# Half of a wo stripe moved ahead of the last V piece and projected there, in a decode-attention kernel

## The chip, the cores and the metric

One core of one Trainium2 chip. The metric is device time in microseconds (us) of one execution; lower is better. "Span" below is the time from the first to the last instruction of an execution; it is 1.2 to 1.6 us (at times up to 2.4 us) shorter than the device time of the same execution, and it was recorded for every run of the experiments.

## The reference

Two independent problems, A and B, of the same shape: one new token per batch row (B = 2), 32 query heads, 16 K/V heads, head size 128, model size 576, a cache of 16384 positions of which only the last W = 4096 count. Everything is bf16.

```python
q = (x @ wq).reshape(B, Sq, Hq, Dh).transpose(0, 2, 1, 3)
k = jnp.repeat(k_cache[:, :, Sk - W:, :], 2, axis=1)
v = jnp.repeat(v_cache[:, :, Sk - W:, :], 2, axis=1)
p = softmax(einsum("bhqd,bhkd->bhqk", q, k) * Dh ** -0.5)
o = einsum("bhqk,bhkd->bhqd", p, v)
out = o.transpose(0, 2, 1, 3).reshape(B, Sq, Hq * Dh) @ wo      # [2, 1, 576]
# the result is A's and B's out, side by side: [2, 1, 1152]
```

The matrix products are tiny, the caches are not: 153 MB have to be read.

## The kernel before

All K and V windows stream through a ring of four 4 MB slots, one slab per (problem, group of four K/V heads, batch row): K slab t, then V slab t - 3, and the pieces of `wo` between them. All large transfers are issued on one queue, in program order. The tail is what is left when the last V slab (number 31) arrives: it is cut into three pieces, and behind it come the last two stripes of `wo`, 6 and 7.

```python
v_cuts = [0, 64, 112, KJ]                 # last V slab: 2048, 1536, 512 KB
w_cuts = [0, 4, 7, 8]                     # stripe 7: 576, 432, 144 KB
# ... (cut)
        stream.append(("V", i))
stream.append(("W", NG - 2))              # stripe 6, one transfer of 1152 KB
stream.append(("W", NG - 1))              # stripe 7, three transfers
# ... (cut)
def filler(n):                            # matmuls whose result nobody reads
    def f(e):
        o = STT[(NG - 1) % 2][:, 0:512]
        last = e.matmul(o, ones_b[:, :], xt[:, 0, 0:512], start=True, stop=True, skip_group_check=True)
        for _ in range(n - 1):
            last = mm_held(e, o, ones_b[:, :], xt[:, 0, 0:512], True)
        return last
    pe(f, [exp_op[NG - 1], Xop[(NSLAB - 1, 1)]], "filler")
# ... (cut)  the tail, in program order:
make_PV(i + 3, (0,))                      # p @ V for piece 0 of the last V slab
make_dg(NG - 1, (0,))                     # selection product: puts heads on partitions
make_pick(NG - 1, (0,))                   # two VectorE steps that finish the attention output
filler(2)
make_PV(i + 3, (1, 2))                    # pieces 1 and 2
make_evac(i + 3)                          # PSUM -> SBUF, then two adds on VectorE
filler(2)
make_dg(NG - 1, (1,))
make_pick(NG - 1, (1,))
make_proj(NG - 2)                         # stripe 6: 8 x 2 matmuls
make_proj(NG - 1)                         # stripe 7: 8 x 2 matmuls; needs the last pick
make_E(NPROB - 1)                         # output
```

The two matmuls of a pair write different partitions (from 0 and from 32) and run side by side: in the trace of before the first two both lie in the 0.40 us from 356.91 us. Stripe 6's product does not need the last pick; stripe 7's does.

## Time and profile before

| | before |
|---|---|
| median of the first three runs | 363.09 us (363.06, 363.09, 364.5) |
| the run that was profiled | 363.97 us, span 362.7 us |
| DMA rate, share | 423 GB/s, engines 90% or more busy in all slices but the first and the last |
| TensorE, VectorE busy | 65%, 58% |

In the slices of the page (each digit is a fortieth of the span, in tenths), the DMA row is full to the end: the kernel is a stream of transfers plus a tail.

```profile
DMA  8999999999999999999999999999999999999995
```

The list of transfers (out and in, queue, operation, count, size, median us from issue to landing) gives their sizes and the time from issue to landing. In this trace the three V pieces were issued at 325.3, 325.9 and 326.5 us and so landed at 349.1, 352.8 and 354.07 us; the four transfers of stripes 6 and 7 were issued from 340.39 to 341.7 us and landed at 356.9, 358.3, 359.35 and 359.7 us.

```profile
wob<-in_B_wo_dram SPq DMA_DIRECT2D x1, 1152.0 KB, 16.5
wob<-in_B_wo_dram SPq DMA_DIRECT2D x1, 576.0 KB, 17.5
ring<-in_B_v_cache_dram SPq DMA_DIRECT2D x1, 512.0 KB, 27.5
```

The chain of waits that ended last, in order of time (start, duration, what), shows the tail: the last V piece, its four matmuls (`ot`), three VectorE steps (left out here, 1.50 us in all), the selection product (`tb`), and 32 projection matmuls (`pj`).

```profile
326.55 27.52 DMA ring<-in_B_v_cache_dram
...
354.12 0.43 PE ot L535 x4
...
356.16 0.79 PE tb L571 x2
356.96 4.00 PE pj L635 x32
...
360.98 0.45 DVE out_sb L651
```

The windows view has one row for a stretch of time: its length, busy time and number of instructions of PE, PEld, DVE, ACT and POOL, then the granted TensorE clock, the DMA share and GB/s.

```profile
351.10:354.50 3.40, 1.21 (x17) 0.38 (x17) 0.26 (x1) 0.00 (x0) 0.00 (x0) 1.00 1.01 418
354.50:357.90 3.40, 2.69 (x18) 1.11 (x15) 2.15 (x5) 0.00 (x0) 0.00 (x0) 0.50 0.98 397
357.90:361.00 3.10, 3.01 (x26) 1.38 (x22) 0.03 (x1) 0.06 (x1) 0.00 (x0) 0.50 0.26 93
```

So the clock was half from 354.5 us on, and the 16 pairs of projection matmuls ran 0.24 us apart, 4.0 us in all, without a wait: stripe 6 had landed at 356.9 us and the selection product ended at 356.95 us.

### The profile page before, as it was taken

How to read it: one execution, taken by the hardware profiler on the slowest of the kernel's cores; microseconds unless marked ns; L12 is line 12 of the kernel's file. 1: busy time of each engine (PE TensorE's matmuls, PEld its weight loads, DVE VectorE, ACT ScalarE, POOL GpSimd, SP SyncE). 2: the span in 40 equal slices, each digit the busy share in tenths (PEclk: the TensorE clock that was granted, in tenths of full speed). 3: DMA queues.
4: the chain of work that ended last, by engine and by line, in shares of the span. 5: the costliest groups of instructions: out<-in, count | busy, mean ns of one | idle time of the engine just before them, and what ended most of it. 6: DMA issues, size and time to landing. Idle time of an engine off the chain costs nothing.

```text
span 362.7 us, 2629 instructions
## 1 busy us (share of the span) xinstructions
PE 237.2 (65%) x1295; PEld 58.2 (16%) x935; DVE 211.9 (58%) x141; ACT 46.2 (13%) x80; POOL 22.1 (6%) x83
## 2 busy tenths in 40 slices
PE   0397687767665868471696666562586677667666
PEld 0010111112111212020131211110112121112222
DVE  0201898495949392924919492942917658585522
ACT  1002100140041001300014001400005000500500
POOL 3100101100010001000010001000010001000000
PEclk9999698969898888986798989889789687889986
DMA  8999999999999999999999999999999999999995
GB/s 326 447 431 416 448 417 441 426 430 437 430 435 408 455 408 426 454 419 444 420 435 426 434 434 414 440 441 412 452 414 442 426 441 420 438 423 441 407 422 220
DMA packets 6228, 153.28 MB, mean 423 GB/s; under 512 B 700, under 2 KB 840, under 8 KB 1224
## 3 DMA queue, kind: packets, MB, share of 16 engines
q1 hardware_dynamic: 6196, 153.10, 98.5%
q8 instruction: 9, 0.15, 0.2%
q10 hardware_dynamic: 20, 0.01, 0.0%
q14 instruction: 3, 0.02, 0.0%
HBM read 153.10 MB, written 0.00 MB: 422 GB/s over the span
## 4 chain that ended last, share of the span: by engine, by line
DMA 48%; DVE 25%; PE 16%; issue 8%; ACT 1%; SPq 0%; POOL 0%; ACTq 0%
DMA ring<-in_B_k_cache_dram 25%; DVE xt L432 15%; DMA ring<-in_A_k_cache_dram 13%; DMA ring<-in_B_v_cache_dram 8%; PE st L248 5%; PE st L458 4%; DMA tmp<-in_B_x_dram 3%; PE pj L248 3%; DVE oR L564 2%; DVE mx L466 2%; DVE pT L505 2%; DVE tmp L557 2%; ACT pR L496 1%; PE ot L279 1%; PE pj L635 1%
## 5 line engine op out<-in xcount | busy, mean ns | idle before, releaser
L458 PE MATMUL st<-xt,zq 128*128 128x512 bf16 x256 | 122.6, 479 | 89.9 <-DVE xt L432 89.8
L432 DVE STREAM_TRANSPOSE xt<-ring 128x4096 f32<-128x4096 f32 x32 | 141.6, 4429 | 36.3 <-DMA ring<-in_A_k_cache_dram 20.8
L248 PE MATMUL st<-xt,zq 128*128 128x512 bf16 x256 | 121.2, 473 | 0.0
L496 ACT ACTIVATE pR<-st,bias 128x512 bf16<-128x512 f32 x32 | 40.0, 1415 | 217.7 <-DVE bias L489 217.7
L458 PEld LDWEIGHTS st<-xt,zq 128*128 128x128 bf16 x256 | 29.0, 113 | 212.7 <-DVE xt L432 106.7
L535 PE MATMUL ot<-ring,pT 128*32 128x512 bf16 x512 | 32.5, 395 | 6.9 <-DMA ring<-in_B_v_cache_dram 4.4
L489 DVE SCALAR_TENSOR_TENSOR bias<-vmask,tb,offm 128x4 f32<-128x4 f32 x8 | 1.8, 223 | 36.1 <-PE tb L486 36.1
L519 DVE TENSOR_REDUCE ssum<-tb 128x2 f32<-128x8 f32 x8 | 1.3, 162 | 36.0 <-PE tb L516 36.0
L505 DVE STREAM_TRANSPOSE pT<-pR 128x2048 bf16<-128x2048 bf16 x8 | 18.4, 2304 | 0.7 <-ACT pR L496 0.7
L424 POOL TENSOR_TENSOR zq<-qs,bmask 128x64 bf16<-128x64 bf16 x32 | 8.6, 292 | 165.7 <-PE st L248 143.8
L557 DVE SCALAR_TENSOR_TENSOR tmp<-ot,rsb,dmask 128x512 f32<-128x512 f32 x16 | 11.5, 719 | 8.5 <-PE ot L535 8.4
L535 PEld LDWEIGHTS ot<-ring,pT 128*32 128x32 bf16 x512 | 12.6, 99 | 22.0 <-DMA ring<-in_B_v_cache_dram 8.9
L564 DVE TENSOR_REDUCE oR<-tmp 128x128 f32<-128x512 f32 x15 | 15.6, 1042 | 0.5
L248 PE MATMUL pj<-ring,pT 128*32 128x512 bf16 x36 | 11.9, 417 | 0.0
L248 PE MATMUL pj<-wob,oM 128*2 128x288 bf16 x48 | 11.9, 286 | 0.0
L616 PE MATMUL pj<-wob,oM 128*2 128x288 bf16 x48 | 11.9, 286 | 0.0
L258 PE MATMUL tb<-ident_b,pR 8*128 8x8 bf16 x9 | 0.7, 198 | 14.5 <-DVE pR L217 14.5
L466 DVE TENSOR_REDUCE mx<-st 128x2 f32<-128x1024 f32 x8 | 9.7, 1214 | 0.1
L496 ACT ACTIVATION_READ_ACCUMULATOR pR<-st,bias 128x1 f32 x32 | 8.9, 278 | 0.0
L217 DVE TENSOR_TENSOR pR<-tmp,hmask 8x1152 bf16<-8x1152 bf16 x1 | 1.3, 1345 | 11.5 <-DMA tmp<-in_B_x_dram 11.5
L279 PE MATMUL ot<-ring,pT 128*32 128x512 bf16 x18 | 7.5, 419 | 0.5 <-ACT pT L265 0.5
L248 PE MATMUL st<-ring,pT 128*32 128x512 bf16 x18 | 7.3, 407 | 0.0
(69 smaller groups left out, 71.4 us busy)
## 6 DMA issues: line engine op xcount, KB each, us to landing
ring<-in_A_k_cache_dram SPq DMA_DIRECT2D x8, 4096.0 KB, 24.9
ring<-in_A_v_cache_dram SPq DMA_DIRECT2D x8, 4096.0 KB, 29.9
ring<-in_B_k_cache_dram SPq DMA_DIRECT2D x8, 4096.0 KB, 28.6
ring<-in_B_v_cache_dram SPq DMA_DIRECT2D x7, 4096.0 KB, 29.9
ring<-in_A_wq_dram SPq DMA_DIRECT2D x1, 4608.0 KB, 13.8
ring<-in_B_wq_dram SPq DMA_DIRECT2D x1, 4608.0 KB, 24.2
wob<-in_A_wo_dram SPq DMA_DIRECT2D x2, 2304.0 KB, 29.8
wob<-in_B_wo_dram SPq DMA_DIRECT2D x1, 2304.0 KB, 27.4
```

Source lines behind the costliest of these rows:

```text
L248: return e.add_instruction(mybir.InstMatmult(name=nc.get_next_instruction_name(), engine=mybir.EngineType.PE, ins=[e.lower_ap(mv_), e.lowe ...
L279: last = e.matmul(QB[c], wt, mv_, start=first, stop=True, skip_group_check=True)
L424: last = e.tensor_tensor(dst, src, msk, ALU.mult)
L432: Xop[(t, jh)] = dve(lambda e: e.transpose(xt[:, jh, :].bitcast(FP32).rearrange("p (kp x kt) -> p x kp kt", kp=2, kt=2), ring[:, r, jh * H ...
L458: last = e.matmul(ob, wt, mv_, start=first, stop=True, skip_group_check=True)
L466: ch[(G, "max")] = dve(lambda e: e.tensor_reduce(mx[:], st[:, :].rearrange("p (x t) -> p t x", t=2), AX.X, ALU.max), [Sop[(2 * G + 1, 1)]] ...
L496: last = e.activation(pR[:].rearrange("p (x k) -> p k x", k=4)[:, kv, :], st[:, :].rearrange("p (x t) -> p t x", t=2)[:, kv % 2, :], ACTF.Exp,
L505: pT_op[G] = dve(lambda e: e.transpose(pT[:, v, :].rearrange("p (w j q) -> p j w q", w=4, q=8), pR[:].rearrange("p (j w q) -> p j w q", w= ...
L535: last = e.matmul(OTB[32 * c:32 * c + 32, :], pT[:, v, base + 32 * c:base + 32 * c + 32], ring[:, r, jj * 128:(jj + 4) * 128], start=rd == ...
L557: evac_op[i] = dve(lambda e: e.scalar_tensor_tensor(tv, o, rsb[:, v, b:b + 1], dm, ALU.mult, ALU.mult), deps, "ev%d" % i)
L564: ch[(G, "red%d" % b)] = dve(lambda e: e.tensor_reduce(oR[:, b, :], tmp[:].rearrange("p (j d) -> p d j", j=4), AX.X, ALU.add), [evac_op[i] ...
L616: last = e.matmul(PJ[h], oM[:, j, :], mv_, start=start and j == 0, stop=True, skip_group_check=True)
```

## The change

The intent, as I read it: VectorE's work after the last V piece leaves TensorE idle (0.71 us ahead of the selection product in the trace of before), and the two filler matmuls ahead of that (1.00 us) do no useful work. Let the first half of stripe 6 arrive ahead of the last V piece and project it there, so that a quarter of the projection leaves the end of the tail.

```diff
+            # order of issue (in ensure): for the last V slab
+                if k == ("V", NSLAB - 1):
+                    issue(k, 0)                 # V pieces 0 and 1
+                    issue(("W", NG - 2), 0)     # stripe 6, first half (576 KB)
+                    issue(k, 1)                 # V piece 2
+                    issue(("W", NG - 2), 1)     # stripe 6, second half
-        stream.append(("W", NG - 2))
@@ the tail
         filler(2)
-        make_PV(i + 3, (1, 2))
+        make_PV(i + 3, (1,))
+        make_proj(NG - 2, (0,))
+        make_PV(i + 3, (2,))
         make_evac(i + 3)
-        filler(2)
         make_dg(NG - 1, (1,))
         make_pick(NG - 1, (1,))
-        make_proj(NG - 2)
+        make_proj(NG - 2, (1,))
         make_proj(NG - 1)
```

(Cut: the bookkeeping that lets a transfer and a projection be asked for in parts, and one more semaphore.)

More of the change, by code (lines that the diff above doesn't have):

```diff
@@ L159, in build_kernel @@
         w_cuts = [0, 4, 7, 8]
-        lastw_sem = [sem("lastw%d" % k) for k in range(2)]
+        lastw_sem = [sem("lastw%d" % k) for k in range(3)]
         wq_sem = [sem("wq%d" % P) for P in range(NPROB)]
@@ L344, in build_kernel, with issue @@
         projm_op = {}
-        def issue(key):
+        def issue(key, part=None):
             kind, i = key
@@ L355, in issue @@
                 cuts = [(0, n, wo_sem[i % 2])]
-                if i == NG - 1:
+                if i == NG - 2 and kind == "W":
+                    cuts = [(0, 4, wo_sem[0]), (4, 8, lastw_sem[2])]
+                if i == NG - 1 and kind == "W":
                     cuts = [(w_cuts[k], w_cuts[k + 1], ([wo_sem[1]] + lastw_sem)[k]) for k in range(3)]
-                stream_dma[key] = []
+                if part is not None:
+                    cuts = cuts[part:part + 1]
+                stream_dma.setdefault(key, [])
                 for j0, j1, sm in cuts:
@@ L373, in issue @@
                 cuts = [(v_cuts[k], v_cuts[k + 1], ([ring_sem[r]] + lastv_sem)[k]) for k in range(3)]
-            stream_dma[key] = []
+                cuts = cuts[0:2] if part == 0 else cuts[2:3]
+            stream_dma.setdefault(key, [])
             for c0, c1, sm in cuts:
@@ L382, in ensure @@
             while key not in stream_dma:
-                issue(stream[pos[0]])
+                k = stream[pos[0]]
                 pos[0] += 1
+                if k == ("V", NSLAB - 1):
[3 more added lines that the diff above has]
+                    issue(("W", NG - 2), 1)
+                else:
+                    issue(k)
         def filler(n):
@@ L621, in make_projm, with make_proj @@
             projm_op[q] = pe(f, deps, "projm%d" % q)
-        def make_proj(G):
+        def make_proj(G, parts=(0, 1, 2)):
             v = G % 2
@@ L626, in make_proj @@
             oPs = [ch[(G, "oP", b)] for b in range(2) if (G, "oP", b) in ch]
-            for j0, j1, dma in stream_dma[("W", G)]:
+            for j0, j1, dma in [x for k, x in enumerate(stream_dma[("W", G)]) if k in parts]:
                 split = G == NG - 1 and j1 == 8
```

## The prediction

> **What bounds the kernel now.** The page's slices show the DMA engines 90% or more busy up to slice 39 at 410-450 GB/s; PE is 65% busy, DVE 58%. The kernel is a DMA stream plus a tail after the last bytes. Only the tail can change; no byte is added.
>
> The chain of waits ends: last V issue 326.5, its data at 354.07, PV 0.43 us, evacuation 0.76, half-sum 0.44, sum 0.30, selection product (dg) 0.79 to 356.95, projection of stripes 6 and 7 as 32 matmuls 4.00 to 360.95, final add 0.45, out. The source view of the DMA issues gives the landings: V pieces 349.1, 352.8, 354.07; stripe 6 (1152 KB) 356.9; stripe 7 358.3, 359.35, 359.7. So stripe 6 and dg release the projection at the same moment. After that PE never waits: 16 pairs start 0.24 us apart, and the windows view shows a granted clock of 0.50 from about 354.5 on. At clock 1.0 one such matmul took 0.12 us in the previous projection (not in pairs).
>
> **What the change does.** The queue's order becomes V piece 1, half of stripe 6, V piece 2, other half, stripe 7. [...] The landings agree (in order of issue, 1.2 us per 512 KB). So:
> - Half of stripe 6 (576 KB at the 1.4 us that stripe 7's first 576 KB took) lands at about 354.2; the last V piece moves 1.4 us later, to about 355.45. The second half and stripe 7 stay. No bubble: V piece 2 now waits behind the stripe's buffer (free at 340.4), with 12 us of V data still queued.
> - 8 of the 32 matmuls (4 pairs, 0.96 us at the half clock) move from after dg into the wait for V, in place of two unused matmuls (1.0 us).
>
> **On the critical path.** After V: 355.45 + PV about 0.55 (now at the half clock; 0.43 before) + 1.50 DVE + dg 0.79 = dg done at about 358.4. The pick takes about 0.75 more, to 359.2, beneath the 4 remaining pairs of stripe 6 (0.96, to 359.4). Stripe 7: 8 pairs, 1.92, to about 361.35. Before: 360.95. The V chain is delayed 1.4 us and gets about 1.0 back: some 0.4 us slower, 0.1%.
>
> **Clock.** [...] the low stretch in the tail is about 6.8 us. The early projection replaces about as much filler as goes, so I expect the half clock to stay. With the full clock, 12 pairs take about 1.45 us and the tail is some 0.8 us shorter.
>
> **Predicted:** 363.4 us, range 362.4 to 364.7 (three runs of before spread 1.4 us). Faster by over 2%: 0.01; within 2%: 0.98; slower: 0.01.
>
> **What would show it.** Landings in the order V1, W6a, V2, W6b, W7 with V2 near 355.4; first 8 projection matmuls at about 354.2; dg ending near 358.4, 1.4 us later; 24 contiguous matmuls after dg, 0.24 apart; the last of them ending near 361.3.
>
> **What would make it wrong.** A different clock in the last 8 us (-0.8 to -1.2 us); split stripe 6 (4.6 KB rows, not 9.2 KB) slowing the stream; a bubble in the queue; the spread of runs, larger than my effect.

(Cut from it: two rules, of the queue and of the clock, that no run of this case shows. No term of its sum goes with them: the selection product done at about 358.4 us and the last matmul at about 361.35, against 360.95 before, so some 0.4 us slower. The order of landings rests on the trace of before, where all seven transfers of the tail landed in the order of issue, from 349.1 to 359.7 us. The 0.55 us for the V matmuls, and that the half clock would stay, were the author's estimates from that trace.)

## The result

The changed kernel took 364.2 us (median of 6 runs, 363.81 to 364.74) against 363.12 us (363.01 to 364.5) for the kernel before: ratio 1.0025, 95% interval 1.0007 to 1.0042. (A ratio here is the mean time of one kernel's fast runs over that of the other's of the same rounds, so it is not quite the ratio of the medians.) That is "the same" at a bar of 2%, inside the predicted range, and on the predicted side of zero. It is about 0.9 us by the means, where 0.3 to 0.4 us was predicted. The predicted range, 362.4 to 364.7 us, also holds a change of nothing, so lying inside it says little about the mechanism.

The slices of the page, as shown of before: the same stream.

```profile
DMA  8999999999999999999999999999999999999995
```

The transfers. The first half of stripe 6 was issued at 341.75 us and landed at 354.14 us; the last V piece, 342.13 and 355.4 us; the second half, 342.71 and 356.8 us; stripe 7's last piece at 359.7 us, as before.

```profile
wob<-in_B_wo_dram SPq DMA_DIRECT2D x3, 576.0 KB, 14.1
...
ring<-in_B_v_cache_dram SPq DMA_DIRECT2D x1, 512.0 KB, 13.3
```

The chain:

```profile
354.94 0.49 PE pj L646 x4
...
355.45 0.43 PE ot L546 x4
...
357.50 0.49 PE tb L582 x2
357.99 3.02 PE pj L646 x14
...
361.03 0.45 DVE out_sb L662
```

And the windows:

```profile
351.10:354.50 3.40, 3.18 (x23) 1.01 (x19) 0.88 (x3) 0.00 (x0) 0.00 (x0) 0.50 1.00 406
354.50:357.90 3.40, 1.73 (x22) 0.74 (x14) 1.47 (x3) 0.00 (x0) 0.00 (x0) 1.00 0.98 391
357.90:361.00 3.10, 3.06 (x25) 1.27 (x24) 0.68 (x2) 0.01 (x1) 0.00 (x0) 0.50 0.24 90
```

Read against the lines of before: the V piece's matmuls start at 355.45 instead of 354.12 us, everything on VectorE is 1.34 us later, the selection product starts at 357.50 instead of 356.16, and 24 instead of 32 matmuls remain behind it. The last of them ends within 0.1 us of where it did. But this comparison is not fair: here the clock was full from 354.5 to 357.9 us, where it was half in the trace of before, so the selection product took 0.49 us against 0.79 us. The two profiled executions (364.01 and 363.97 us) do not show the difference that the medians show. Where it lies had to be found by experiment.

### The profile page after: what moved, and what is told of

It reads as the page before. It is cut to its first block, busy times and chain, and to the rows that moved or that the text cites. A ratio compares the mean times of both kernels' runs of the same rounds, so it can differ in the third digit from the quotient of the medians.

```text
span 362.8 us, 2626 instructions
## 1 busy us (share of the span) xinstructions
PE 231.4 (64%) x1292; PEld 57.6 (16%) x934; DVE 211.8 (58%) x141; ACT 46.3 (13%) x80; POOL 22.2 (6%) x83
## 4 chain that ended last, share of the span: by engine, by line
DMA 49%; DVE 24%; PE 17%; issue 8%; ACT 1%; POOL 0%; ACTq 0%
DMA ring<-in_B_k_cache_dram 25%; DVE xt L443 13%; DMA ring<-in_A_k_cache_dram 13%; DMA ring<-in_B_v_cache_dram 8%; PE st L248 4%; PE pj L248 3%; DMA tmp<-in_B_x_dram 3%; PE ot L546 3%; PE st L469 2%; DVE mx L477 2%; DVE oR L575 2%; DVE pT L516 2%; DVE tmp L568 2%; ACT pR L507 1%; PE ot L279 1%
## 5 line engine op out<-in xcount | busy, mean ns | idle before, releaser
L469 PE MATMUL st<-xt,zq 128*128 128x512 bf16 x256 | 118.5, 463 | 93.2 <-DVE xt L443 93.2
L248 PE MATMUL st<-xt,zq 128*128 128x512 bf16 x256 | 117.1, 457 | 0.0
L469 PEld LDWEIGHTS st<-xt,zq 128*128 128x128 bf16 x256 | 28.2, 110 | 210.2 <-DVE xt L443 110.0
L546 PE MATMUL ot<-ring,pT 128*32 128x512 bf16 x512 | 35.3, 420 | 7.4 <-DMA ring<-in_B_v_cache_dram 3.9
L279 PE MATMUL ot<-ring,pT 128*32 128x512 bf16 x18 | 7.4, 410 | 0.5 <-ACT pT L265 0.5
```

The costliest lines, as they stand in the source:

```text
L248: return e.add_instruction(mybir.InstMatmult(name=nc.get_next_instruction_name(), engine=mybir.EngineType.PE, ins=[e.lower_ap(mv_), e.lowe ...
L279: last = e.matmul(QB[c], wt, mv_, start=first, stop=True, skip_group_check=True)
L469: last = e.matmul(ob, wt, mv_, start=first, stop=True, skip_group_check=True)
L546: last = e.matmul(OTB[32 * c:32 * c + 32, :], pT[:, v, base + 32 * c:base + 32 * c + 32], ring[:, r, jj * 128:(jj + 4) * 128], start=rd == ...
```

## The experiments

Three theories were on the table.
- "Order": the last V piece lands 1.4 us later and only part of that comes back.
- "Stream": the extra transfer and the shorter rows cost.
- "Fillers" or "clock": the order costs little; what counts is whether the tail gets the full clock, and the filler matmuls that went set the odds.

Each of the three groups of four below ran on one chip, in 5 rounds together with the kernel before. As the part of the device time outside the span differed by up to 1.2 us between runs (1.2 to 2.4 us), I quote spans too. The four numbers are: median device time, ratio to before with its interval, mean span, mean span of before in the same rounds.

| run | what | median us | ratio (95%) | span | span before |
|---|---|---|---|---|---|
| a1_after_again | changed kernel | 364.0 | 1.0011 (0.9996 to 1.0025) | 362.57 | 362.22 |
| a2_order_only | transfers as changed, matmuls as before | 365.45 | 1.0046 (1.0026 to 1.0066) | 363.75 | 362.22 |
| a3_cut_only | stripe 6 cut, order as before | 363.54 | 1.0 (0.9987 to 1.0014) | 362.25 | 362.22 |
| a4_v_first_half_early | V first, half of stripe 6 early | 363.28 | 0.9994 (0.9982 to 1.0006) | 362.00 | 362.22 |
| b1_after_filler_back | changed, fillers back | 363.32 | 0.9994 (0.9976 to 1.0013) | 362.27 | 362.27 |
| b2_before_full_clock | before, 30 fillers | 363.13 | 0.9985 (0.9971 to 0.9999) | 361.98 | 362.27 |
| b3_after_full_clock | changed, 30 fillers | 363.29 | 0.9989 (0.9975 to 1.0003) | 362.08 | 362.27 |
| b4_filler_removed_only | before, second fillers gone | 363.2 | 0.9987 (0.9973 to 1.0002) | 362.04 | 362.27 |
| c1_after_third | changed kernel | 364.04 | 1.0015 (1.0 to 1.0029) | 362.72 | 362.11 |
| c2_after_filler_back_again | changed, fillers back | 363.59 | 1.0012 (0.9997 to 1.0027) | 362.40 | 362.11 |
| c3_order_only_full_clock | a2 with 30 fillers | 364.57 | 1.0018 (1.0002 to 1.0034) | 362.95 | 362.11 |
| c4_whole_stripe_ahead_full_clock | all of stripe 6 ahead, 30 fillers | 364.76 | 1.0045 (1.003 to 1.0061) | 363.83 | 362.11 |

All twelve gave the correct result.

### a1_after_again

No edit: the changed kernel again. (By the rival "clock" below, executions differ only in when the clock is half.)

> The changed kernel again, unaltered, for a second trace and the width of its noise beside the three variants. Theory 'order' (the last V piece lands 1.4 us later and only part of that is given back by the 8 matmuls that leave the tail): 0.3 to 1.2 us over the kernel before, the last V piece landing near 355.4 in the profile. Rival 'clock' [...]: the sign changes from run to run, mean difference under 0.2 us.

Measured: ratio 1.0011, 0.35 us by spans. The six runs lie at 363.28, 363.35, 363.69, 364.32, 364.36 and 364.53 us, and the profiled one is the lowest. Its tail had the full clock from 354.94 us to the end and its last matmul ended at 360.26 us, 0.74 us ahead of the profile above (361.00 us). Two of its windows, in the columns given above:

```profile
351.50:354.90 3.40, 3.18 (x23) 1.01 (x19) 0.81 (x3) 0.00 (x0) 0.00 (x0) 0.50 0.98 395
354.90:358.30 3.40, 1.75 (x26) 0.90 (x20) 1.54 (x4) 0.00 (x0) 0.00 (x0) 0.99 0.96 383
```

So one and the same kernel ends at different levels (below, the "upper level" is runs over 363.9 us), and the clock of the tail differs between these two profiles. The mean difference stayed positive and is at the low end of what "order" expected; the last V piece landed at 355.6 us.

### a2_order_only

```diff
-        make_PV(i + 3, (1,))
-        make_proj(NG - 2, (0,))
-        make_PV(i + 3, (2,))
+        make_PV(i + 3, (1, 2))
         make_evac(i + 3)
+        filler(2)
         make_dg(NG - 1, (1,))
         make_pick(NG - 1, (1,))
-        make_proj(NG - 2, (1,))
+        make_proj(NG - 2)
```

> The changed order of transfers (half of stripe 6 ahead of the last V piece), but the projection all after the last pick and the filler matmuls back, as before. Theory 'order': the V chain is 1.4 us late and nothing is given back, so 1.0 to 1.8 us over the kernel before, and slower than the changed kernel by 0.5 to 1.0 us. Rival 'fillers' (the changed kernel lost because its filler matmuls are gone): no slower than the kernel before by more than 0.3 us. Rival 'stream' (one more transfer, rows of 4.6 KB): 0.3 to 1 us slower with the last piece of stripe 7 landing later than 359.8.

Measured: 1.5 us over before by spans, 1.7 us by the ratio; 1.2 us slower than the changed kernel, rather more than the 0.5 to 1.0 us that was expected. TensorE's timeline (start, duration, engine, line, operation, operands, count, idle time before and its cause):

```profile
355.68 0.62 PE L546 MATMUL ot<-ring,pT 128*32 128x512 bf16 x4 [1.88 <-DMA ring<-in_B_v_cache_dram]
...
357.94 0.79 PE L582 MATMUL tb<-oR,selx 128*128 128x128 f32 x2 [0.67 <-DVE oR L571]
358.67 3.19 PE L646 MATMUL pj<-wob,oP 128*2 128x288 bf16 x32
```

The V piece is waited for until 355.68 us and the selection product ends at 358.73 us, 1.8 us later than in the trace of before. Its stripe 7 had landed by 359.9 us, 0.2 us after before's, and did not hold anything up. So the order of transfers with the matmuls left behind the pick costs, the early matmuls earn most of it back, and "fillers" cannot be the whole story, because the fillers are here. How much of the 1.5 us is lateness and how much the half clock (from 354.06 to 360.88 us in this profile) the run does not separate: five of its six spans are 363.7 to 364.3 us, the sixth is 362.2 us, which is the lower level of the kernel before.

### a3_cut_only

```diff
                     issue(k, 0)
-                    issue(("W", NG - 2), 0)
                     issue(k, 1)
+                    issue(("W", NG - 2), 0)
                     issue(("W", NG - 2), 1)
```
(with the matmuls of a2)

> Stripe 6 in two halves as in the change, but both behind the last V piece; matmuls as before. Theory 'order': within 0.2 us of the kernel before. Rival 'stream' (the extra cut is what costs): 0.3 to 1 us slower, like the changed kernel.

Measured: ratio 1.0, span 362.25 against 362.22 us. One more transfer and 4.6 KB rows cost nothing that can be seen: "stream" is out as what the change costs. But its profiled run, at the upper level, had not only the half clock: its whole stream was late, the last V piece landing at 354.74 us and stripe 7 at 360.41 us, both 0.7 us after before's (stripe 7 landed at 359.7 us in the profile of the changed kernel, 359.85 in b2 and 359.9 in a2). So the clock is not the only thing that makes a run long.

### a4_v_first_half_early

```diff
 (transfers as in a3)
         make_evac(i + 3)
         filler(2)
+        make_proj(NG - 2, (0,))
         make_dg(NG - 1, (1,))
         make_pick(NG - 1, (1,))
-        make_proj(NG - 2)
+        make_proj(NG - 2, (1,))
```

> The last V piece keeps its place ahead of stripe 6; the first half of stripe 6 lands right behind it (about 355.5) and is projected ahead of the last selection product, where the tensor engine was idle waiting for the vector engine. Theory 'order': the 0.96 us of matmuls leaves the tail at no cost to V, selection product done near 357.2, stripe 7 bound by its own landings, end 0.3 to 0.8 us ahead of the kernel before. If taking matmuls out of the tail is worth nothing (the tail bound by stripe 7's landing alone): within 0.2 us of the kernel before.

Measured: 0.2 us below before, interval across zero: smaller than expected. The timeline of its profiled run, at full clock, says why:

```profile
355.67 0.65 PE L646 MATMUL pj<-wob,oP 128*2 128x288 bf16 x8 [0.49 <-DMA wob<-in_B_wo_dram]
356.29 0.49 PE L582 MATMUL tb<-oR,selx 128*128 128x128 f32 x2
357.11 0.65 PE L646 MATMUL pj<-wob,oP 128*2 128x288 bf16 x8 [0.33 <-DMA wob<-in_B_wo_dram]
358.60 0.66 PE L646 MATMUL pj<-wob,oP 128*2 128x288 bf16 x8 [0.84 <-DMA wob<-in_B_wo_dram]
359.58 0.65 PE L646 MATMUL pj<-wob,oP 128*2 128x288 bf16 x8 [0.32 <-DMA wob<-in_B_wo_dram]
```

Every group of projection matmuls waits for its transfer (`<-DMA wob`). In this run, at full clock, the tail is bound by the landings of stripe 7 (the last eight matmuls start at 359.58 us, after 0.32 us of waiting), and taking matmuls out of it earns nothing. Its five runs all lie between 363.14 and 363.63 us, without the upper level that the kernel before shows.

### b1_after_filler_back

```diff
         make_evac(i + 3)
+        filler(2)
         make_dg(NG - 1, (1,))
```
(on the changed kernel)

> The changed kernel with the two filler matmuls put back where they stood, between the last evacuation and the last selection product. Theory 'order' (late V piece): nothing much changes, 0.3 to 1.0 us over the kernel before. Rival 'fillers' (the tail runs at the half clock more often because 1 us of matmuls is gone): at or below 363.6 us, within 0.2 us of the kernel before.

Measured: five runs at 363.08 to 363.46 and one at 364.73 us, mean span equal to before's (362.27). This is what "fillers" expected, but with six runs it needed a second look (c2).

### b2_before_full_clock

```diff
+        filler(8)
         make_PV(i + 2)
         make_evac(i + 2)
+        filler(8)
 ...
         make_pick(NG - 1, (0,))
-        filler(2)
+        filler(7)
         make_PV(i + 3, (1, 2))
         make_evac(i + 3)
-        filler(2)
+        filler(7)
```

> The kernel before with 30 filler matmuls in the idle stretches of the last 20 us, so that the tail should run at full clock in every run. The earlier runs suggest that the kernel before ends at two levels: near 363.2 when its tail has the full clock (then bound by the landings of stripe 7) and near 364.2 when it has the half clock. Theory: full clock in the tail of the profile, matmuls of stripe 7 waiting for their transfers, times all at 363.0 to 363.5 without the upper level, 0 to 0.4 us below the kernel before on average. If the two levels come from elsewhere (the transfers): the spread stays.

Measured: 363.12, 363.12, 363.13, 363.23 and 363.47 us; spans 361.9 to 362.2. The 11 runs of before beside them have spans of 361.8 to 363.0. The upper level went away, as expected. In the profile the tail is at full clock and waits for its transfers:

```profile
356.17 0.49 PE L571 MATMUL tb<-oR,selx 128*128 128x128 f32 x2
356.93 1.14 PE L635 MATMUL pj<-wob,oP 128*2 128x288 bf16 x16 [0.27 <-DMA wob<-in_B_wo_dram]
358.44 0.65 PE L635 MATMUL pj<-wob,oP 128*2 128x288 bf16 x8 [0.36 <-DMA wob<-in_B_wo_dram]
359.38 0.80 PE L635 MATMUL pj<-wob,oP 128*2 128x288 bf16 x8 [0.29 <-DMA wob<-in_B_wo_dram]
```

### b3_after_full_clock

The same edit on the changed kernel (with `filler(7)` where b1 has `filler(2)`).

> The changed kernel with the same filler matmuls. At full clock the delay of the V chain (1.4 us) leaves the pick at about 358.7 and the last matmul at about 360.2, where the landing of stripe 7 allows about 360.0 to 360.3. Theory 'order and clock' (the late V chain hurts only as far as the clock is half behind it): 363.1 to 363.6, within 0.3 us of the full-clock kernel before. Theory 'order alone': still 0.5 us or more over the full-clock kernel before.

Measured: 363.27 to 363.64 us, mean span 362.08: 0.10 us over b2, which is within the spread of the five runs of each. With the clock held full, the change costs about 0.1 us at most.

```profile
357.69 0.49 PE L582 MATMUL tb<-oR,selx 128*128 128x128 f32 x2
358.11 0.65 PE L646 MATMUL pj<-wob,oP 128*2 128x288 bf16 x8
358.98 1.27 PE L646 MATMUL pj<-wob,oP 128*2 128x288 bf16 x16 [0.21 <-DVE oP L612]
359.60 0.40 PEld L646 LDWEIGHTS pj<-wob,oP 128*2 128x2 bf16 x8 [0.29 <-DMA wob<-in_B_wo_dram]
```

Here the last 16 matmuls start when the pick is done (`<-DVE oP`); among them only the last eight weight loads (PEld) still wait for a transfer of stripe 7, 0.29 us. The late V piece has used up nearly all the slack that stripe 7's landing left, and the end is 360.25 us where b2 has 360.18.

### b4_filler_removed_only

```diff
         make_evac(i + 3)
-        filler(2)
         make_dg(NG - 1, (1,))
```
(on the kernel before)

> The kernel before without its second pair of filler matmuls, nothing else. Rival 'fillers': 0.4 to 1.0 us over the kernel before, the tail at the half clock more often. Theory 'order': within 0.2 us of the kernel before.

Measured: 363.06 to 363.75 us, mean span 362.04 against 362.27 us of before. In the old order the fillers' removal costs nothing: against "fillers" as a general rule. If it matters, then only together with the new order.

### c1_after_third and c2_after_filler_back_again

c1 is the changed kernel, c2 is b1; no other edit.

> The changed kernel a third time, beside the next run on one chip, to see how many of its runs end at the upper level (over 363.9 us; so far 7 of 12 against 8 of 28 of the kernel before). Theory 'fillers set the odds of the half clock': half or more of its runs at the upper level. Rival 'chance': about as many as of the kernel before in the same rounds.

> The changed kernel with the two filler matmuls put back, again, on the chip of the run ahead. Theory 'fillers set the odds of the half clock': at most 2 of 6 runs over 363.9 us, 0.3 us or more below the changed kernel on average. Rival 'chance': as the changed kernel within 0.2 us.

Measured: c1 has three of six runs over 363.9 us (of before, one of eleven), c2 two of six, so the counts went as "fillers" expected. The means did not: c2 is 0.10 us below c1 by device time, which is the rival's range. By spans it is 0.32 us (362.40 against 362.72), as one of c2's two high runs, 364.76 us, has a span of 362.4 us: 2.4 us of it lay outside the instructions. That reading was chosen afterwards; taken together, the pair does not decide.

The profiled run of c1 (364.26 us) shows a tail of the upper level. Its windows, in the columns given above:

```profile
353.90:357.30 3.40, 1.42 (x20) 0.36 (x12) 1.09 (x2) 0.00 (x0) 0.00 (x0) 1.00 1.01 407
357.30:360.70 3.40, 2.94 (x22) 1.65 (x24) 1.05 (x4) 0.00 (x0) 0.00 (x0) 0.50 0.36 142
```

TensorE's timeline of the same stretch:

```profile
355.72 0.40 PE L546 MATMUL ot<-ring,pT 128*32 128x512 bf16 x4 [0.62 <-DMA ring<-in_B_v_cache_dram]
357.76 0.80 PE L582 MATMUL tb<-oR,selx 128*128 128x128 f32 x2 [1.65 <-DVE oR L571]
358.49 2.72 PE L646 MATMUL pj<-wob,oP 128*2 128x288 bf16 x24
```

In the stretch from 353.9 to 357.3 us, TensorE was busy for 1.42 of 3.40 us, as it had nothing to do between the last V matmuls and the selection product (idle 1.65 us). The clock halved at 357.33 us, and the selection product (0.80 us) and most of the 24 matmuls (2.72 us, to 361.2 us) ran at half clock, which lasted to 360.75 us. In b1, with the fillers in that gap, the same stretch was busy for 2.12 us and the clock stayed full to the end. The windows of b1:

```profile
353.70:357.10 3.40, 2.12 (x26) 0.46 (x13) 0.78 (x2) 0.00 (x0) 0.00 (x0) 1.00 1.03 413
357.10:360.50 3.40, 2.26 (x26) 1.08 (x26) 1.44 (x5) 0.11 (x1) 0.00 (x0) 1.00 0.44 170
```

### c3_order_only_full_clock

a2 with the edit of b2.

> Order of transfers as changed, the projection all behind the last pick as in the order-only kernel (which was 1.7 us slower than before), plus the filler matmuls of the full-clock kernels. If the late V piece costs only where the clock is half: selection product done near 358.1, 32 matmuls in 2 us, end near 360.3, 363.2 to 363.7 us, within 0.4 us of the full-clock kernel before. If lateness costs one for one at any clock: 1.2 us or more over it.

Measured: two runs at 363.24 and 363.4 us, four at 364.53 to 364.76. The fillers did not do what they were put there for: in the profiled run the clock halved at 356.23 us, in the middle of them, and the last six of the seven fillers took 2.75 us and themselves held up the selection product:

```profile
356.22 2.75 PE L248 MATMUL st<-xt,ones_b 128*128 128x512 bf16 x6
358.76 0.64 PE L582 MATMUL tb<-oR,selx 128*128 128x128 f32 x2
359.33 2.26 PE L646 MATMUL pj<-wob,oP 128*2 128x288 bf16 x32
```

So as a test of lateness at full clock the run failed. The two low runs are in line with "late V is harmless at full clock", but no profile of them exists.

### c4_whole_stripe_ahead_full_clock

```diff
 (b3, and)
                     issue(k, 0)
                     issue(("W", NG - 2), 0)
-                    issue(k, 1)
                     issue(("W", NG - 2), 1)
+                    issue(k, 1)
 ...
-        make_proj(NG - 2, (0,))
+        make_proj(NG - 2, (0, 1))
 ...
-        make_proj(NG - 2, (1,))
```

> The whole of stripe 6 ahead of the last V piece and projected there, with the filler matmuls of the full-clock kernels: V another 1.4 us later (near 357.0), selection product done near 359.5, pick near 360.2, the 16 matmuls of stripe 7 to 361.5. If at full clock the V chain had about 1.2 to 1.4 us of slack that the change used up: 364.2 to 364.8 us, 1.0 to 1.4 us over the full-clock changed kernel. If stripe 7's landing bounds the tail all the same: within 0.4 us of it.

Measured: 364.54 to 366.1 us; the profiled run, at full clock throughout the tail, has a span of 363.4 us, 1.3 us over b3's. (Four of its six runs lie there, two 1.2 us higher; those two have no profile. By medians it is 1.47 us over b3, measured on another chip, just above the 1.0 to 1.4 us expected.)

```profile
359.16 0.49 PE L582 MATMUL tb<-oR,selx 128*128 128x128 f32 x2
360.45 1.15 PE L646 MATMUL pj<-wob,oP 128*2 128x288 bf16 x16 [0.80 <-DVE oP L612]
```

The V matmuls start at 357.12 us, 1.47 us after b3's 355.65, and the last matmul ends 1.35 us later. This second half stripe is paid nearly one for one, while the first cost 0.1 us. At full clock there was about as much slack as the change uses: the 0.12 us that c4 does not pay is what b3 had left.

## Why the prediction was right or wrong

**Order of landings: right.** The transfers landed in the order of issue, as in the trace of before. V piece 2 was predicted at 355.45 us and landed at 355.4, the first half of stripe 6 at 354.2 (354.14), stripe 7 unchanged at 359.7. The stream did not slow (a3, ratio 1.0) and no bubble opened.

**The trade: right in sign and mechanism.** The prediction's sum was made for the half clock, and there the traces bear it out: in c1 the V matmuls start 1.60 us later than in the profile of before (355.72 against 354.12 us) and the last matmul ends 0.30 us later (361.21 against 360.91 in the timelines, with c1's clock full again for its last 0.46 us), where 1.4 and 0.4 were predicted. By mean spans late V costs 1.5 us (a2 against before), and the matmuls moved forward (with the two fillers gone, too) earn 1.2 us of it back (a1 against a2). That these means leave about the predicted 0.3 to 0.4 us is in part luck: they mix executions at the half and at the full clock, and at the full clock the trade costs about 0.1 us at most (b3 against b2).

**Clock: the step that failed.** The prediction wrote: "The early projection replaces about as much filler as goes, so I expect the half clock to stay." It took the half clock of the one trace for the kernel's normal state (though it did name another clock, worth 0.8 to 1.2 us, among what would make it wrong). Half probably is not the normal state. The spans of the kernel before suggest that it usually runs its tail at full clock; its one profile is of the upper level, so this is seen only in its near variants b2 and b4. Those of its 33 runs beside the experiments begin at 361.8 us, 22 of them are at most 362.3, and 11 lie above, as did the profiled run at 362.7 us. In the profiles of a1, a4, b1, b2, b3, b4 and c2 the clock was full behind the last V piece, and the last projection matmul ended between 360.2 and 360.6 us; in those of before, a3, c1 and the changed kernel's first it was half for 3 us or more of what follows that piece, and it ended between 360.9 and 361.6 us (a2, c3 and c4, whose tails are bound otherwise, are left out). Of the changed kernel only 6 of 18 runs are at most 362.3 us (the cut at 362.3 is mine; the two groups are not cleanly apart).

So the measured difference has two parts. The mean span of the changed kernel (18 runs) is 362.74 us, that of before 362.20 us (33 runs), a difference of 0.54 us.
- Level: among the runs above 362.3 us, the changed kernel's mean is 363.08 us and that of before 362.70 us, so 0.4 us, the size predicted for the half clock. Among the lower runs it is about 0.1 us, the size of b3 against b2.
- Odds: 12 of 18 runs are above that cut, against 11 of 33. Weighting with these shares, the shift from one third to two thirds at about 0.75 to 1 us between levels is worth some 0.3 us: the part that was not predicted. This split is an estimate: the cut was chosen afterwards, spans also differ by the stream (a3), and with so few runs shares of 12 in 18 and 11 in 33 differ only just beyond chance.

**What sets the odds is not settled.** The traces of c1 and b1 show how a gap without matmuls behind the last V piece precedes the half clock, and how fillers in it went with the full clock (1.42 and 2.12 us busy of 3.40 us). In the last 20 us the half clock lasted 3.41 us (from 344.28 us) and 6.82 us (from 354.52) in the trace of before, and 10.24 us (from 344.28) and 3.41 us (from 357.93) in the first of the changed kernel; so I compare stretches of 3.41 us that begin at a clock change. In the three profiles of the changed kernel TensorE was busy for 1.40 us (c1), 1.74 us (the first) and 1.76 us (a1) in the stretch that holds the gap (a few hundredths off the stretches shown above); the clock halved after the first two and stayed full after the third. With the fillers back it was busy for 2.11 (b1) and 2.29 us (c2), and the clock stayed full. Putting the fillers back also brought the mean span from 362.74 (18 runs) to 362.33 us (12 runs, b1 and c2). That favours the missing fillers.

Against it: the kernel before without the same fillers (b4) lost nothing in five runs (1.76 us in its profile, and the clock stayed full), and on one chip c1 and c2 differ by 0.3 us with overlapping intervals. And in the profile of before the half clock follows another gap, the wait for the last V pieces (1.23 us busy from 351.11 to 354.52 us), into which the changed kernel puts its early matmuls. When the clock changed differed between executions (in the last 20 us first at 344.28 us in the profile of before, 343.82 in a2, 345.75 in a4), and with it what such a stretch holds. What makes the clock change is not shown, so the odds need many more runs than these.

**The spread of runs** was named as larger than the effect, and was.

**A version that beats both?** b2, the kernel before with more fillers, is the lowest by mean, 0.15% below before with an interval (0.9971 to 0.9999) that just excludes zero, and without the upper level. b4 and a4 lie as low within the noise. None is near 2%: at full clock the end is fixed by stripe 7's last landing (359.85 us in b2, where the last matmul ended at 360.18 us).

## What to carry to other kernels

Here, in a stream on one queue, moving 576 KB forward moved the V piece that it overtook back by 1.3 us (355.4 against 354.07 us), and 576 KB more in c4 moved it by another 1.47 us. At full clock the first cost 0.1 us at most, as the V piece had slack, and the second nearly all of its time (1.35 us), so find first what the end of the tail waits for. Before reading a tail from one trace, compare that run's time with the median: a trace from the upper level shows costs (here 32 matmuls at half clock in 4.00 us, and no slack) that most runs seem not to have. Matmuls that nobody reads may be worth keeping (not settled here), but they sit in order ahead of the critical product; in c3, where the clock halved under them, the last six took 2.75 us and held it up (1.46 us in b3).
